# Staging of the first weights, row maxima of v and the route of two early blocks in an attention and MLP kernel

## The chip, the cores and the metric

The kernel runs on one core of one Trainium2 chip. The metric is the device time of one execution in microseconds; lower is better. The five engines are named as in the profile: PE (TensorE, matrix products), DVE (VectorE), ACT (ScalarE), POOL (GpSimd) and SP (SyncE, which issues nearly all of the DMAs).

## The reference

Four batches of eight heads, 768 positions of 64 numbers, go through a local attention, and its output goes through an MLP with 512 inputs, 2048 hidden columns and 512 outputs. All inputs are 32-bit floats except the two MLP weights, which come as 64-bit floats.

```
scores = scale * q @ k.T - slope[h] * dist          # 96 positions back, and the first 8
a = exp(scores - max) / (sum + 1e-9)
x = (a @ v), heads side by side                       # 3072 x 512
h = x @ w_in;  g = h / (1 + exp(-h));  out = g @ w_out
```

## The kernel before

**Blocks.** The 3072 positions are 24 blocks of 128 rows (six to a batch). For each block the kernel loads q, k and v, and the 96 rows of v before it with the first 8 (`vp`); it transposes q and k on PE, computes scores for the block's 232 columns (128 for the first block of a batch), adds the bias and takes the maximum on DVE (line 617), the exponential with its sum on ACT (line 625), transposes P on PE (line 650), copies it back on ACT (line 656) and multiplies with v. A pair of heads is one step; four pairs make a block. The blocks' outputs x are split into a high and a low part of reduced precision (`xh`, `xl`, lines 715 and 718), so that three fast products stand for one exact one.

**Two routes.** Blocks below `IV` (6) leave P as it is: `values_q` (line 677) makes x with positions as rows, the whole block is divided by its sums (`guard_all`, `inverse_all`, `norm_all`), and `turn_x` transposes it. Other blocks divide P before its transposes (`guard`, `inverse`, `norm`, lines 630 to 641), and `values` (line 670) gives x transposed at once, for all four pairs in one run from block `I0` (6) on. From that block on scores too are made of split halves ("stacked", line 578).

**MLP.** Three blocks form a group of 384 columns. Its hidden layer is 16 chunks f of 128 columns, each twelve products (line 833), then tanh on ACT (839), the gate on DVE (843) and a write to DRAM (848). After the eight groups, pairs of blocks are read back, and the output layer is made by seven products on sums and differences (line 888).

**Weights.** w_in arrives as 16 pieces of 512 KB, one for each chunk, in tiles `ws` with seven buffers (tags z0 to z6). DVE makes 32-bit numbers of the 64-bit ones in three operations (365, 371, 377), ACT rounds the high part (383) and DVE subtracts it (387). Each chunk has a tile `wi` of its own, whose memory the output layer uses again (`PART`, `HL`, `OUT`, line 850). w_out follows in eight pairs, whose high and low parts are one operation each (lines 398 to 421), over the memory of the first weights.

**Checks.** The fast route holds for inputs within limits. DVE finds the row maxima of v (`scale_of`, line 511) for each block right after its load, and reads both weights a second time for their extremes (line 473); a verdict at the end decides whether the general route runs.

**Order.** The order of all instructions is found while the program is built. A planner (`Plan`) holds each operation with engine, estimated cost, rank, predecessors and buffers; on each engine it takes, when the engine is free, the ready operation of lowest rank. Where PE has nothing ready in the planner's first 60 us it inserts a filler, a product of zeros (line 1103). Each engine then runs its queue in that fixed order and waits on semaphores. Rank counts pairs of heads: block i's scores have ranks 4 i to 4 i + 3, its loads of q and k 4 i - 8.5 and of v 4 i - 7.5. The conversion of chunk n has rank `C0` + n, its load that less `LW` (12). Hidden-layer products have ranks above 1000 and so go behind attention; tanh, gate and write go ahead of everything. Attention from block 7 on waits for hidden-layer products of earlier groups (`AHEAD`).

Of the kernel before, what the change touches and what calls it, by code (L numbers as in the profile page):

```python
# [21 lines left out]
P = 128  # L22
# [149 lines left out]
def attn_moe(ctx, tc, q, k, v, n_global, n_local, w_in, w_out, out):  # L172
# [176 lines left out]
    def stage(n, nm):  # L349
        if nm == "w" and n < NFC:  # L350
            t = const.tile([P, 3 * 512], U32, name=f"ws_{n}", tag=f"z{n % 7}")
            st["f", n] = t[:, 1024:]
            x = t[:, :1024].rearrange("p (f w) -> p f w", w=2)
        else:
            x = sbx.tile([P, 512, 2], U32, name=f"{nm}_{n}", tag="big")
# [41 lines left out]

    def pair_hi(p):
        if p < 3:
            x = [const.tile([P, 7, HM], F32R, name=f"wo_{p}_{i}", tag=f"z{2 * p + i}") for i in range(2)]  # L400
        elif p < HF - 1:
            x = [st["late"].tile([P, 7, HM], F32R, name=f"wo_{p}_{i}") for i in range(2)]
        else:
            x = [sbx.tile([P, 6, HM], F32R, name=f"wo_{p}_{i}", tag=("xh", "xl")[i]) for i in range(2)]
            y = st["late"].tile([P, 2, HM], F32R, name="wo_last")
            w2[p, 0, 6], w2[p, 1, 6] = y[:, 0], y[:, 1]
        for i in range(2):
            for c in range(7):
                w2.setdefault((p, i, c), x[i][:, c] if c < x[i].shape[1] else None)
        st["wo", p] = x  # L410
        n = x[0].shape[1]
        nc.scalar.copy(x[0], st["F", p][:, :n])
        if n < 7:
            nc.scalar.copy(w2[p, 0, 6], st["F", p][:, 6])

    def pair_lo(p):
        x = st["wo", p]
        n = x[0].shape[1]
        nc.vector.tensor_sub(x[1], st["F", p][:, :n], x[0].bitcast(F32))
        if n < 7:  # L420
            nc.vector.tensor_sub(w2[p, 1, 6], st["F", p][:, 6], w2[p, 0, 6].bitcast(F32))
# [18 lines left out]
    for p in range(HF):  # L440
# [17 lines left out]
        hi = op("ACT", ACT(7 * HM), rank, (lambda p=p: pair_hi(p)), [o] + ([o_late] if p > 2 else []), [F, *a])  # L458
        lo = op("DVE", DVE(7 * HM), rank, (lambda p=p: pair_lo(p)), [hi], [F, *a])
        o_w2.append((hi, lo))  # L460

# [14 lines left out]

    o_c, o_cd, cbuf, o_vm = [], [], [], []
    for n in range(2 * NFC):
# [247 lines left out]
    for i in range(B * NJ):  # L726
# [50 lines left out]
        for hp in range(NHP):  # L777
# [29 lines left out]
            if not plain:  # L807
                last = op("PE", 900 if j else 450, u - PAR["RV"], (lambda i=i, hp=hp, av=pav: values_q(i, hp, av)),
                          [o_m.pop(), last] + o_v, [pt, pav, kk["vn"]] + ([kk["vp"]] if j else []))
            elif not stacked or hp == NHP - 1:  # L810
                last = op("PE", ((2100 if j else 1250) if stacked else 726 if j else 508), u - PAR["RV"],
                          (lambda i=i, hp=hp, av=pav: values_of(i, hp, av)),
                          [*o_m, last] + o_v, [*pts, pav, xb[g]["xh"], xb[g]["xl"], kk["vn"]] + ([kk["vp"]] if j else []))
                o_m, pts = [], []
# [14 lines left out]
    def moe_h(g, f, c, h):  # L829
        mo["ph", g, f] = ph = bank(h, GT)  # L830
        xh, xl = xt["xh", g], xt["xl", g]
        for n, (w, x) in enumerate(((0, xh), (0, xl), (1, xh))):
            nc.tensor.matmul(  # L833
                ph, w1[f][:, w, c], x[:, c], start=not c and not n, stop=c == NCC - 1 and n == 2
            )
# [13 lines left out]

    PART, HL, OUT = ((0, 3, 6, 7), (12, 13, 14, 15)), ((1, 2), (4, 5), (8, 9)), (10, 11)  # L850

    def quarter(g, n):
        t, k = divmod(n, 2)
        b, j = divmod(2 * g + t, NB)
        mo["a", g, n] = x = const.tile([P, HF, P], F32, name=f"a_{g}_{n}", tag=f"wi{PART[g % 2][n]}")
        nc.sync.dma_start(x, gate[b][:, j, k * HF:(k + 1) * HF])
# [17 lines left out]
    def split_hi(g, m):  # L874
        r = HL[(7 * g + m) % len(HL)]
        x = [const.tile([P, HF, P], F32R, name=f"g{i}_{g}_{m}", tag=f"wi{r[i]}") for i in range(2)]
        mo["hl", g, m] = x
        nc.scalar.copy(x[0], mo["a", g, PROD[m][0]])  # L878

    def split_lo(g, m):  # L880
        x = mo["hl", g, m]
        nc.vector.tensor_sub(x[1], mo["a", g, PROD[m][0]], x[0].bitcast(F32))  # L882

    def product(g, m, p, po):
        mo["po", g, m] = y = bank(po, HM)
        a, c = mo["hl", g, m], PROD[m][1]
        for n, (i, w) in enumerate(((0, 0), (0, 1), (1, 0))):
            nc.tensor.matmul(  # L888
                y, a[i][:, p], w2[p, w, c], start=not p and not n, stop=p == HF - 1 and n == 2,
            )  # L890

    def place(g, n):
        if ("out", g) not in mo:
            mo["out", g] = const.tile([P, 2, 2, HM], F32, name=f"o_{g}", tag=f"wi{OUT[g % 2]}")
        return mo["out", g][:, n // 2, n % 2]
# [13 lines left out]

    def moe_out(g, t):  # L910
        n = 2 * g + t
        nc.sync.dma_start(out[n * P:(n + 1) * P], mo["out", g][:, t].rearrange("p a c -> p (a c)"))

    o_h, o_put = {}, {}
    FIRST = -1e6
    for g in range(NGRP):
        o = o_h[g - 1, NFC - 1] if g else None
        for f in range(NFC):
            rank = 1e3 + g * NFC + f
            ph, th = Buf("h"), Buf("g1")  # L920
# [10 lines left out]
    def was(*tags):  # L931

        return [o_h[NGRP - 1, x] for x in tags]

# [4 lines left out]
    for g in range(NPAIR):  # L939
# [4 lines left out]
        for n in range(4):  # L944
            b = (2 * g + n // 2) // NB
            o_q.append(op("DMA", 1456, rank - 8, (lambda g=g, n=n: quarter(g, n)),
                          [o_put[b, NFC - 1]] + (was(PART[g][n]) if first else [free_q[g - 2][n]]), [gq[n]], PAR["DL"]))
        ob, E, ev = Buf("ob"), Buf("g1"), {}
        for m, (src, c) in enumerate(PROD):
# [8 lines left out]
            if not g and src == 0:  # L958
# [4 lines left out]
            hi = op("ACT", ACT(1024), r, (lambda g=g, m=m: split_hi(g, m)),  # L963
                    [h0, o_spl.get("hi")] + (was(*HL[m]) if not g and m < len(HL) else []), [*used, hl])
            o_spl["hi"] = hi
# [10 lines left out]
            if m in (0, 3):  # L976
                ev[m] = op("ACT", ACT(HM), e, (lambda g=g, m=m: keep_half(g, m)),
                           [o] + (was(*OUT) if not g else []), [po, E if m else ob])
            elif m == 1:
                o_1, po_1 = o, po  # L980
            else:
# [297 lines left out]
```

## Time and profile before

| | |
|---|---|
| median of 3 runs (lowest to highest) | 709.94 us (709.85 to 710.8) |
| the profiled execution | 710.94 us |
| its span | 709.2 us |
| PE, PE weight load | busy 694.5 us (98%), 664.6 us (94%) |
| DVE, ACT, POOL | busy 590.5 us (83%), 425.1 us (60%), 26.1 us (4%) |
| mean granted TensorE clock | 0.997 of 2.4 GHz |
| DMA | 114.32 MB, mean 161 GB/s |

The span runs from the first to the last instruction of the profiled execution. A busy time is the union of an engine's instructions; products are pipelined, so the mean of one in a group (346 ns for 384 columns) is longer than its share of the time. Attention and hidden layer share the first 400 us, the hidden layer alone goes on to 463 us, and the output layer takes the rest.

### The profile page before, as it was taken

The numbers are of one execution on the slowest core, as the hardware profiler recorded it, in microseconds if no ns is written. First come the engines' busy times: TensorE is split into PE (matmuls) and PEld (weight loads), VectorE is DVE, ScalarE is ACT, GpSimd is POOL, SyncE is SP. The second block draws the span as 40 slices with busy tenths as digits, with TensorE's granted clock in tenths as the row PEclk, the third lists the DMA queues.
The fourth block names the chain that finished last, engine by engine and source line by source line (L and its number), as shares of the span: only waits on it lengthen the run. The fifth ranks groups of instructions, "written<-read, shape, count | busy, mean of one in ns | idle before, by whom it ended". The sixth has DMA issues, their size and how long they took to land.

```text
span 709.2 us, 14385 instructions
## 1 busy us (share of the span) xinstructions
PE 694.5 (98%) x5294; PEld 664.6 (94%) x5294; DVE 590.5 (83%) x1416; ACT 425.1 (60%) x938; POOL 26.1 (4%) x81
## 2 busy tenths in 40 slices
PE   8999998999999999999999999999999999999996
PEld 5889898998999999999998999999999999999996
DVE  4999798897777888777798558889989899988893
ACT  5877884877777787777797634443333433343331
POOL 2000100000000000000010000000000000000000
PEclk9999999999999999999999999999999999999999
DMA  8979885644566566566542277776544554455300
GB/s 193 266 172 218 180 203 155 177 112 127 139 169 161 139 168 162 134 163 171 137 124 77 71 208 223 228 241 197 196 134 167 188 172 171 147 195 178 121 31 34
DMA packets 175469, 114.32 MB, mean 161 GB/s; under 512 B 96544, under 2 KB 162080, under 8 KB 175392
## 3 DMA queue, kind: packets, MB, share of 16 engines
q1 hardware_dynamic: 175104, 113.34, 56.6%
q8 instruction: 43, 0.70, 0.4%
q14 instruction: 34, 0.28, 0.1%
q10 hardware_dynamic: 288, 0.00, 0.0%
HBM read 81.86 MB, written 31.46 MB: 160 GB/s over the span
## 4 chain that ended last, share of the span: by engine, by line
PE 83%; DVE 9%; ACT 5%; DMA 2%; issue 1%; SPq 0%; DVEq 0%
PE bank L888 34%; PE bank L833 32%; PE bank L650 4%; PE bank L670 4%; PE bank L578 3%; PE bank L518 2%; ACT pe L625 1%; DMA vn<-in_v_dram 1%; PE bank L684 1%; DVE pe L617 1%; PE bank L1103 1%; PE bank L602 1%; DVE th L843 1%; DVE ws L371 1%; DVE ws L377 1%
## 5 line engine op out<-in xcount | busy, mean ns | idle before, releaser
L833 PE MATMUL bank<-xh,wi 128*128 128x384 f32 x1024 | 293.3, 346 | 0.2 <-DVE KL L565 0.2
L888 PE MATMUL bank<-wo,g 128*128 128x256 f32 x1980 | 237.5, 281 | 0.0
L888 PEld LDWEIGHTS bank<-wo,g 128*128 128x128 f32 x1980 | 235.9, 189 | 0.0
L833 PEld LDWEIGHTS bank<-xh,wi 128*128 128x128 f32 x1024 | 188.7, 189 | 3.3 <-issue 2.5
L833 PE MATMUL bank<-xl,wi 128*128 128x384 f32 x512 | 173.1, 338 | 0.0
L625 ACT ACTIVATE pe<-pe,NM 128x232 f32<-128x232 f32 (+1 forms) x192 | 90.2, 471 | 33.0 <-DVE NM L617 31.9
L833 PEld LDWEIGHTS bank<-xl,wi 128*128 128x128 f32 x512 | 97.1, 190 | 0.0
L839 ACT ACTIVATE th<-bank 128x384 f32<-128x384 f32 x128 | 62.1, 487 | 50.9 <-PE bank L833 50.2
L878 ACT CAST g<-S 128x1024 fp32r<-128x1024 f32 x48 | 49.9, 1049 | 61.0 <-DVE S L868 36.3
L843 DVE SCALAR_TENSOR_TENSOR th<-th,bank 128x384 f32<-128x384 f32 x128 | 69.8, 548 | 12.0 <-ACT th L839 11.5
L617 DVE CUSTOM_DVE_ANT_0 pe<-bank,B 128x232 f32<-128x232 f32 (+1 forms) x192 | 67.2, 374 | 12.0 <-PE bank L578 6.7
L882 DVE TENSOR_TENSOR g<-S,g 128x1024 fp32r<-128x1024 f32 x48 | 58.4, 1220 | 15.0 <-ACT g L878 14.9
L650 PE MATMUL bank<-ident,pe 128*128 128x128 f32 (+1 forms) x352 | 57.4, 278 | 5.4 <-DVE pe L641 4.5
L878 ACT CAST g<-a 128x1024 fp32r<-128x1024 f32 x36 | 37.8, 1050 | 37.2 <-PE bank L888 35.2
L656 ACT COPY pt<-bank 128x512 f32<-128x512 f32 (+1 forms) x96 | 52.0, 544 | 7.8 <-PE bank L650 7.4
L650 PEld LDWEIGHTS bank<-ident,pe 128*128 128x128 f32 (+1 forms) x352 | 40.9, 136 | 15.3 <-DVE pe L641 7.5
L473 DVE TENSOR_REDUCE TOP<-c 128x1 f32<-128x512 int16 x64 | 42.3, 677 | 6.4 <-DMA c<-in_moe_w_in_dram 6.2
L882 DVE TENSOR_TENSOR g<-a,g 128x1024 fp32r<-128x1024 f32 x36 | 43.9, 1219 | 3.3 <-ACT g L878 3.2
L641 DVE TENSOR_SCALAR pe<-pe,rs 128x232 f32<-128x232 f32 (+1 forms) x144 | 41.7, 331 | 1.2
L625 ACT ACTIVATION_READ_ACCUMULATOR pe<-pe,NM 128x1 f32 x192 | 36.4, 189 | 0.0
L903 DVE SCALAR_TENSOR_TENSOR o<-bank,o 128x256 f32<-128x256 f32 x60 | 25.1, 419 | 9.3 <-PE bank L888 8.8
L868 DVE TENSOR_TENSOR S<-a,a 128x1024 f32<-128x1024 f32 x24 | 29.3, 1220 | 0.7 <-PE bank L833 0.5
(134 smaller groups left out, 855.1 us busy)
## 6 DMA issues: line engine op xcount, KB each, us to landing
gate<-th SPq DMA_DIRECT2D x128, 192.0 KB
a<-gate SPq DMA_DIRECT2D x48, 512.0 KB
ws<-in_moe_w_in_dram SPq DMA_DIRECT2D x16, 512.0 KB
w<-in_moe_w_out_dram SPq DMA_DIRECT2D x16, 512.0 KB
c<-in_moe_w_in_dram SPq DMA_DIRECT2D x16, 512.0 KB
c<-in_moe_w_out_dram SPq DMA_DIRECT2D x16, 512.0 KB
vn<-in_v_dram SPq DMA_DIRECT2D x24, 256.0 KB
out_dram<-o SPq DMA_DIRECT2D x24, 256.0 KB
```

The lines of the kernel that those rows point to most:

```text
L473: nc.vector.tensor_reduce(TOP[:, i, n:n + 1], top, AX.X, (ALU.min, ALU.max)[i], apply_absolute_value=True)
L617: nc.vector.tensor_tensor_reduce(t["p", hp][:, a, :n], t["s", hp][a][:, :n], B1[:, h] if i % NJ else B0[:, h], -SC, 3.0e38, ALU.add, ALU.m ...
L625: nc.scalar.activation(x, x, AF.Exp, bias=NM[:, i * H + h:i * H + h + 1], scale=-1.0, accum_out=t["sum", hp][:, a:a + 1],)
L641: nc.vector.tensor_scalar(x, x, t["inv", hp][:, a:a + 1], None, ALU.mult)
L650: nc.tensor.transpose(ps[:n, c, a], pe[:, a, c0:c0 + n], ident)
L656: nc.scalar.copy(t["pt", hp][:, c], t["tp", hp][:, c])
L833: nc.tensor.matmul(ph, w1[f][:, w, c], x[:, c], start=not c and not n, stop=c == NCC - 1 and n == 2)
L839: nc.scalar.activation(th, mo["ph", g, f], AF.Tanh, scale=0.5)
L843: nc.vector.scalar_tensor_tensor(gf, gf, 1.0, mo["ph", g, f], ALU.add, ALU.mult)
L878: nc.scalar.copy(x[0], mo["a", g, PROD[m][0]])
L882: nc.vector.tensor_sub(x[1], mo["a", g, PROD[m][0]], x[0].bitcast(F32))
L888: nc.tensor.matmul(y, a[i][:, p], w2[p, w, c], start=not p and not n, stop=p == HF - 1 and n == 2,)
```

## The change

- w_in comes in eight pieces of 1 MB, two chunks each, in tiles of three buffers (tags y0 to y2, 12 KB a partition). Each conversion operation has 1024 columns where it had 512, and a tile `wi` holds two chunks. Conversion ranks become 14, 16, ... 28, and those of their loads 0, 2, ... 14.
- The memory that the first weights leave is cut anew: w_out pairs 0 to 2 take y0 to y2; `PART`, `HL` and `OUT` name the wider tiles, and the two output tiles become one tile of two halves.
- The high and low parts of a w_out pair are made in two operations each, of four and three columns of 256.
- `IV` becomes 4: blocks 4 and 5 divide P before its transposes, and their values come in one run at the block's end.
- The row maxima of v for blocks 0 to 5 are taken from a second load of v (`again`), which starts behind hidden-layer products of groups 2 to 4. For other blocks the maximum has rank 4 i + 3 and is put behind the exponentials of the third pair.
- The last output rows leave as two DMAs, one for each half of the columns.

```diff
-    C0=8, CR=1, LW=12, LB=5, QB=3.5, RI=0.1, RN=0, RP=0.2, RM=0, RV=1.2, RQ=0.1, RB=3, LK=-25,
-
-    BP=(4, 3), CF=8, AHEAD=5, CN=19, I0=6, IV=6, QS='ACT', O0=14, ON=16, PF=16,
+    C0=14, CR=1, LW=14, LB=5, QB=3.5, RI=0.1, RN=0, RP=0.2, RM=0, RV=1.2, RQ=0.1, RB=3, LK=-25,
+
+    BP=(4, 3), CF=8, AHEAD=5, CN=19, I0=6, IV=4, QS='ACT', O0=14, ON=16, PF=16,
...
+    def stage2(n):
+
+        t = const.tile([P, 3 * 1024], U32, name=f"ws_{n}", tag=f"y{n % 3}")
+        st["f", n] = t[:, 2048:]
+        st["w", n] = x = t[:, :2048].rearrange("p (f w) -> p f w", w=2)
+        src = w_in.bitcast(U32).rearrange("(c p) (f w) -> p c f w", p=P, w=2)[:, :, 2 * n * P:2 * (n + 1) * P]
+        nc.sync.dma_start(x.rearrange("p (c f) w -> p c f w", c=NCC), src)
...
+    CUT = (slice(0, 4), slice(4, 7))
+
+    def pair_hi(p, half):
+        if not half:
+            pair_home(p)
+        x, F, c = st["wo", p][0], st["F", p], CUT[half]
+        if x.shape[1] < c.stop:
+            nc.scalar.copy(w2[p, 0, 6], F[:, 6])
+            c = slice(c.start, 6)
+        nc.scalar.copy(x[:, c], F[:, c])
...
-    for n in range(NFC):
-        rank = PAR["C0"] + PAR["CR"] * n
-        o = op("DMA", 2000, rank - PAR["LW"], (lambda n=n: stage(n, "w")), [o_w[n - 7][1]] if n > 6 else (), (), PAR["DW"])
-        o = op("DVE", 335, rank, (lambda n=n: conv1(n)), [o])
-        o = op("DVE", 602, rank, (lambda n=n: conv2(n)), [o])
-        o = op("DVE", 602, rank, (lambda n=n: conv3(n)), [o])
-        hi = op("ACT", 520, rank, (lambda n=n: conv_hi(n)), [o])
-        lo = op("DVE", 602, rank, (lambda n=n: conv_lo(n)), [hi])
+    for n in range(HF):
+        rank = PAR["C0"] + 2 * PAR["CR"] * n
+        o = op("DMA", 3600, rank - PAR["LW"], (lambda n=n: stage2(n)), [o_w[n - 3][1]] if n > 2 else (), (), PAR["DW"])
+        o = op("DVE", 602, rank, (lambda n=n: conv1(n)), [o])
+        o = op("DVE", 1135, rank, (lambda n=n: conv2(n)), [o])
+        o = op("DVE", 1135, rank, (lambda n=n: conv3(n)), [o])
+        hi = op("ACT", ACT(1024, 90), rank, (lambda n=n: conv_hi(n)), [o])
+        lo = op("DVE", 1135, rank, (lambda n=n: conv_lo(n)), [hi])
...
     def scale_of(i):
+        x = st["v", i] if i < PAR["I0"] else blk[i]["v"]
         nc.vector.tensor_reduce(
-            VM[:, i:i + 1], blk[i]["v"].rearrange("p h d -> p (h d)"), AX.X, ALU.max, apply_absolute_value=True
+            VM[:, i:i + 1], x.rearrange("p h d -> p (h d)"), AX.X, ALU.max, apply_absolute_value=True
         )
+
+    def again(i):
+        b, j = divmod(i, NJ)
+        st["v", i] = sbx.tile([P, H, D], F32, name=f"va_{i}", tag="big")
+        nc.sync.dma_start(st["v", i], v[b, :, j * P:(j + 1) * P, :].rearrange("h p d -> p h d"))
...
-        for x in range(NHP) if i >= PAR["I0"] else (hp,):
+        for x in range(NHP):
             values(i, x, av)
...
-        o_vm.append(op("DVE", 602, NHP * i + 2, (lambda i=i: scale_of(i)), list(o_v), [kk["vn"]]))
+        va = Buf("big") if i < PAR["I0"] else kk["vn"]
+        o_va = [op("DMA", 1456, 2e6 + i, (lambda i=i: again(i)), (), [va], PAR["DL"])] if i < PAR["I0"] else list(o_v)
+        o_vm.append(op("DVE", 602, 1e6 if i < PAR["I0"] else NHP * i + 3, (lambda i=i: scale_of(i)), o_va, [va]))
+        o_va2.append((o_va[0], o_vm[-1]))
...
+            if hp == NHP - 2 and i >= PAR["I0"]:
+                plan.after(o_va2[i][1], *o_e)
...
-    PART, HL, OUT = ((0, 3, 6, 7), (12, 13, 14, 15)), ((1, 2), (4, 5), (8, 9)), (10, 11)
+    PART, HL, OUT = ((0, 3), (6, 7)), (1, 2, 4), 5
...
+                    last = g == NPAIR - 1 and m == 6
+                    op("DMA", 728, e, (lambda g=g, t=m - 5, h=0 if last else None: moe_out(g, t, h)), [ev[m], ev[1]], [ob], PAR["DO"])
+                    if last:
+                        op("DMA", 364, e, (lambda g=g: moe_out(g, 1, 1)), [ev[7]], [ob], PAR["DO"])
...
+    for i in range(PAR["I0"]):
+        plan.after(o_va2[i][0], o_h[divmod(2 * NFC + 2 + 8 * i, NFC)])
```

## Rows read from the trace of the kernel before

**Rows 1.** The page's first part: busy us of each engine, share of the span, instructions.

```profile
PE 694.5 (98%) x5294; PEld 664.6 (94%) x5294; DVE 590.5 (83%) x1416; ACT 425.1 (60%) x938; POOL 26.1 (4%) x81
```

**Rows 2.** All engines in stretches of 20 us: us of the stretch; busy us and instructions of PE, PE weight load, DVE, ACT and POOL; granted clock, DMA share, GB/s.

```profile
20.00:40.00 20.00, 20.00 (x176) 17.40 (x175) 19.80 (x54) 15.83 (x45) 1.04 (x2) 1.00 1.09 261
40.00:60.00 20.00, 19.73 (x150) 17.11 (x148) 19.90 (x55) 15.45 (x41) 1.24 (x3) 1.00 0.63 157
60.00:80.00 20.00, 20.00 (x147) 17.93 (x147) 19.37 (x54) 15.75 (x41) 1.32 (x4) 1.00 1.07 226
80.00:100.00 20.00, 19.05 (x131) 17.43 (x130) 15.97 (x53) 19.52 (x53) 1.26 (x4) 1.00 0.82 197
```

**Rows 3.** The same stretches, line 1103 (the fillers) alone: busy us and instructions of PE and PE weight load, clock, DMA share, GB/s.

```profile
20.00:40.00 20.00, 7.37 (x50) 4.66 (x50) 1.00 1.09 261
40.00:60.00 20.00, 1.44 (x9) 0.51 (x6) 1.00 0.63 157
```

**Rows 4.** Pieces of the chain that ended last: start us, length us, what (x how many).

```profile
35.50 1.73 PE bank L684 x16
...
37.67 0.94 PE bank L1103 x8
...
42.41 0.60 DVE xl L718
...
57.25 0.60 DVE xl L718
...
166.46 0.44 PE bank L650 x4
...
172.75 1.91 PE bank L670 x32
...
194.60 2.12 PE bank L833 x12
```

**Rows 5.** Stretches of 20 us, line 387 (the last operation of a chunk's conversion) alone: busy us and instructions of DVE, clock, DMA share, GB/s.

```profile
20.00:40.00 20.00, 3.86 (x6) 1.00 1.09 261
40.00:60.00 20.00, 3.78 (x6) 1.00 0.63 157
```

**Rows 6.** The stretch 40 to 60 us, line 833 (hidden-layer products) alone: busy us and instructions of PE and PE weight load, clock, DMA share, GB/s.

```profile
40.00:60.00 20.00, 8.42 (x37) 6.07 (x38) 1.00 0.63 157
```

**Rows 7.** Who waited for whom between 100 and 170 us: us in total, times, longest us.

```profile
PE bank L650 <- DVE pe L641: 3.4, 3, 1.9
...
DVE VM L511 <- DMA vn<-in_v_dram: 2.6, 2, 1.4
```

**Rows 8.** Pieces of the chain around the two stalls: start us, length us, what.

```profile
113.18 5.17 DMA vn<-in_v_dram
...
119.97 0.26 DVE pe L641
...
156.62 5.01 DMA vn<-in_v_dram
```

**Rows 9.** All engines in stretches of 2 us, columns as in rows 2.

```profile
118.00:120.00 2.00, 0.39 (x3) 0.07 (x1) 1.63 (x7) 1.09 (x1) 0.00 (x0) 1.00 0.45 144
120.00:122.00 2.00, 1.72 (x9) 1.61 (x10) 2.00 (x5) 1.90 (x6) 0.00 (x0) 0.85 0.31 99
122.00:124.00 2.00, 2.00 (x9) 2.00 (x9) 2.00 (x6) 0.40 (x1) 0.00 (x0) 0.50 0.03 8
124.00:126.00 2.00, 2.00 (x11) 2.00 (x11) 2.00 (x9) 0.45 (x2) 0.00 (x0) 0.80 0.31 100
```

**Rows 10.** DVE's groups of instructions by line and shape: line, operation, out<-in, partitions x elements, count; busy us, mean ns of one; idle before them, and what ended it.

```profile
L882 DVE TENSOR_TENSOR g<-a,g 128x1024 fp32r<-128x1024 f32 x36 | 43.9, 1219 | 3.3 <-ACT g L878 3.2
...
L641 DVE TENSOR_SCALAR pe<-pe,rs 128x232 f32<-128x232 f32 x120 | 35.9, 341 | 1.0
...
L511 DVE TENSOR_REDUCE VM<-vn 128x1 f32<-128x512 f32 x24 | 16.3, 681 | 5.7 <-DMA vn<-in_v_dram 5.6
...
L632 DVE TENSOR_SCALAR rs<-sm 128x2 f32<-128x2 f32 x72 | 12.0, 168 | 17.8 <-ACT pe L625 17.5
...
L371 DVE SCALAR_TENSOR_TENSOR ws<-ws 128x512 uint32<-128x512 uint32 x16 | 11.2, 706 | 0.2
...
L377 DVE SCALAR_TENSOR_TENSOR ws<-ws 128x512 uint32<-128x512 uint32 x16 | 10.9, 683 | 0.1
...
L387 DVE TENSOR_TENSOR wi<-ws,wi 128x512 fp32r<-128x512 f32 x16 | 10.7, 684 | 0.4 <-ACT wi L383 0.4
...
L365 DVE TENSOR_SCALAR ws<-ws 128x512 uint32<-128x512 uint32 x16 | 6.5, 411 | 0.0
```

**Rows 11.** ACT's groups, columns as in rows 10.

```profile
L878 ACT CAST g<-a 128x1024 fp32r<-128x1024 f32 x36 | 37.8, 1050 | 37.2 <-PE bank L888 35.2 <-DMA a<-gate 2.0
...
L383 ACT CAST wi<-ws 128x512 fp32r<-128x512 f32 x16 | 9.8, 621 | 2.3 <-DVE ws L377 2.0
```

**Rows 12.** Who DVE waited for between 175 and 345 us: us in total, times, longest us.

```profile
DVE TOP L473 <- DMA c<-in_moe_w_in_dram: 6.2, 5, 1.7
```

**Rows 13.** Who PE waited for in the whole span, its loads: us in total, times, longest us.

```profile
PE bank L518 <- DMA qn<-in_q_dram: 1.0, 1, 1.0
PE bank L518 <- DMA kn<-in_k_dram: 0.6, 1, 0.6
```

**Rows 14.** The last piece of the chain: start us, length us, what.

```profile
703.49 0.42 DVE o L903
```

**Rows 15.** All engines in one stretch at the end, columns as in rows 2.

```profile
705.00:706.00 1.00, 0.00 (x0) 0.00 (x0) 0.00 (x0) 0.00 (x0) 0.00 (x0) 1.00 0.54 199
```

More of the change, by code (lines that the diff above doesn't have):

```diff
@@ L349, in stage @@
     def stage(n, nm):
[L350 to L355, printed above, removed]
+        x = sbx.tile([P, 512, 2], U32, name=f"{nm}_{n}", tag="big")
         st[nm, n] = x
         nc.sync.dma_start(x if n >= NFC else x.rearrange("p (c f) w -> p c f w", c=NCC), source(n))
+    def stage2(n):
[4 more added lines that the diff above has]
+        nc.sync.dma_start(x.rearrange("p (c f) w -> p c f w", c=NCC), src)
     def conv1(n):
@@ L396, in combine, with pair_home @@
         nc.vector.tensor_sub(F[:, x], F[:, a], F[:, b])
-    def pair_hi(p):
+    def pair_home(p):
         if p < 3:
-            x = [const.tile([P, 7, HM], F32R, name=f"wo_{p}_{i}", tag=f"z{2 * p + i}") for i in range(2)]
+            t = const.tile([P, 2, 7, HM], F32R, name=f"wo_{p}", tag=f"y{p}")
+            x = [t[:, i] for i in range(2)]
         elif p < HF - 1:
@@ L407, in pair_hi @@
         for i in range(2):
-            for c in range(7):
-                w2.setdefault((p, i, c), x[i][:, c] if c < x[i].shape[1] else None)
+            for c in range(x[0].shape[1]):
+                w2[p, i, c] = x[i][:, c]
         st["wo", p] = x
[L411 to L421, printed above, removed]
@@ new lines, in pair_hi, with pair_lo @@
+    def pair_hi(p, half):
[6 more added lines that the diff above has]
+        nc.scalar.copy(x[:, c], F[:, c])
+    def pair_lo(p, half):
+        x, F, c = st["wo", p], st["F", p], CUT[half]
+        if x[0].shape[1] < c.stop:
+            nc.vector.tensor_sub(w2[p, 1, 6], F[:, 6], w2[p, 0, 6].bitcast(F32))
+            c = slice(c.start, 6)
+        nc.vector.tensor_sub(x[1][:, c], F[:, c], x[0][:, c].bitcast(F32))
@@ L457, in attn_moe @@
                 x.left = 1
-        hi = op("ACT", ACT(7 * HM), rank, (lambda p=p: pair_hi(p)), [o] + ([o_late] if p > 2 else []), [F, *a])
-        lo = op("DVE", DVE(7 * HM), rank, (lambda p=p: pair_lo(p)), [hi], [F, *a])
-        o_w2.append((hi, lo))
+        his, los = [], []
+        for i in range(2):
+            n = (4, 3)[i] * HM
+            his.append(op("ACT", ACT(n), rank, (lambda p=p, i=i: pair_hi(p, i)), [o, *his] + ([o_late] if p > 2 else []), [F, *a]))
+            los.append(op("DVE", DVE(n), rank, (lambda p=p, i=i: pair_lo(p, i)), [his[-1]], [F, *a]))
+        o_w2.append(los)
     def size_of(n):
@@ L475, in check @@
         )
-    o_c, o_cd, cbuf, o_vm = [], [], [], []
+    o_c, o_cd, cbuf, o_vm, o_va2 = [], [], [], [], []
     for n in range(2 * NFC):
@@ L809, in attn_moe @@
                           [o_m.pop(), last] + o_v, [pt, pav, kk["vn"]] + ([kk["vp"]] if j else []))
-            elif not stacked or hp == NHP - 1:
-                last = op("PE", ((2100 if j else 1250) if stacked else 726 if j else 508), u - PAR["RV"],
+            elif hp == NHP - 1:
+                last = op("PE", 2100 if j else 1250, u - PAR["RV"],
                           (lambda i=i, hp=hp, av=pav: values_of(i, hp, av)),
@@ L833, in moe_h @@
             nc.tensor.matmul(
-                ph, w1[f][:, w, c], x[:, c], start=not c and not n, stop=c == NCC - 1 and n == 2
+                ph, w1[f // 2][:, w, c, f % 2 * P:(f % 2 + 1) * P], x[:, c], start=not c and not n, stop=c == NCC - 1 and n == 2
             )
@@ L888, in product @@
             nc.tensor.matmul(
-                y, a[i][:, p], w2[p, w, c], start=not p and not n, stop=p == HF - 1 and n == 2,
+                y, a[:, i, p], w2[p, w, c], start=not p and not n, stop=p == HF - 1 and n == 2,
             )
@@ L893, in place @@
         if ("out", g) not in mo:
-            mo["out", g] = const.tile([P, 2, 2, HM], F32, name=f"o_{g}", tag=f"wi{OUT[g % 2]}")
+            if g < 2:
+                st["out"] = st["out"] if g else const.tile([P, 2, 2, 2, HM], F32, name="o", tag=f"wi{OUT}")
+            mo["out", g] = st["out"][:, g % 2]
         return mo["out", g][:, n // 2, n % 2]
@@ L908, in add_kept, with moe_out @@
         nc.vector.tensor_add(x[:, 1::2], x[:, 1:3], st["E", g].unsqueeze(1).to_broadcast([P, 2, HM]))
-    def moe_out(g, t):
-        n = 2 * g + t
-        nc.sync.dma_start(out[n * P:(n + 1) * P], mo["out", g][:, t].rearrange("p a c -> p (a c)"))
+    def moe_out(g, t, half=None):
+        n, c = 2 * g + t, slice(0, 2) if half is None else slice(half, half + 1)
+        nc.sync.dma_start(
+            out[n * P:(n + 1) * P, c.start * HM:c.stop * HM], mo["out", g][:, t, c].rearrange("p a c -> p (a c)")
+        )
     o_h, o_put = {}, {}
@@ L931, in was @@
     def was(*tags):
-        return [o_h[NGRP - 1, x] for x in tags]
+        return [o_h[NGRP - 1, 2 * x + 1] for x in tags]
     o_p, sx = [], [Buf("xh"), Buf("xl")]
@@ L946, in attn_moe @@
             o_q.append(op("DMA", 1456, rank - 8, (lambda g=g, n=n: quarter(g, n)),
-                          [o_put[b, NFC - 1]] + (was(PART[g][n]) if first else [free_q[g - 2][n]]), [gq[n]], PAR["DL"]))
+                          [o_put[b, NFC - 1]] + (was(PART[g][n // 2]) if first else [free_q[g - 2][n]]), [gq[n]], PAR["DL"]))
         ob, E, ev = Buf("ob"), Buf("g1"), {}
@@ L963, in attn_moe @@
             hi = op("ACT", ACT(1024), r, (lambda g=g, m=m: split_hi(g, m)),
-                    [h0, o_spl.get("hi")] + (was(*HL[m]) if not g and m < len(HL) else []), [*used, hl])
+                    [h0, o_spl.get("hi")] + (was(HL[m]) if not g and m < len(HL) else []), [*used, hl])
             o_spl["hi"] = hi
@@ L977, in attn_moe @@
                 ev[m] = op("ACT", ACT(HM), e, (lambda g=g, m=m: keep_half(g, m)),
-                           [o] + (was(*OUT) if not g else []), [po, E if m else ob])
+                           [o] + (was(OUT) if not g else []), [po, E if m else ob])
             elif m == 1:
```

15 lines of the change are left out of this document (8 added, 7 removed).

## The prediction

> **What bounds the kernel now.** I read the busy table first: TensorE (PE) is busy 694.5 of 709.2 us, so 14.7 us of the whole span show it idle [rows 1]. That is not all that it loses, because some of its busy time is filler: the multiplications of zeros that the kernel issues (line 1103) where its planner saw PE with nothing to do. So the next view was the first 100 us in stretches of 20 us [rows 2]. Between 20 and 80 us PE and VectorE (DVE) are both full, DVE at 19.8, 19.9 and 19.4 of 20 us; ScalarE (ACT) has about 4 us spare in each stretch until 80 us and none between 80 and 100. The same stretches for line 1103 alone show 50 fillers between 20 and 40 us and 9 between 40 and 60 [rows 3]. A run of 8 takes 0.94 us on the chain [rows 4], so 50 x 0.1175 = 5.9 us of the second stretch are filler: there DVE can't feed PE, as it does weight conversion and attention at once. From 40 us on PE has useful work nearly always: by 60 us some 12 chunks of w_in are split while only 37 hidden-layer multiplications, three chunks' worth, have run [rows 5, 6]. That is a lead of nine chunks, 9 x 12 x 0.177 = 19 us of PE work (12 take 2.12 us [rows 4]). So from 40 us what counts is PE's own work and the few places where its queue stands still.
>
> The largest such places are two waits for DVE. PE waits for the normalised P (line 641) 3.4 us between 100 and 170 us, and DVE waits in the same stretch 2.6 us for v to land, with the row maximum of v (line 511) at the head of its queue [rows 7]. The chain shows both: v takes 5.17 and 5.01 us from issue to landing, and the row maximum stands at its end [rows 8]. After the first of them PE's granted clock falls: 0.85, 0.50 and 0.80 in the three stretches of 2 us from 120 us, after PE did 0.39 us of work in 118 to 120 [rows 9]. At a clock of 0.50, half of the time is lost: 0.3 + 1.0 + 0.4 = 1.7 us. The two places cost some 3.4 + 1.7 = 5.1 us.
>
> **The change part by part.**
>
> Blocks 4 and 5 by the later blocks' route. Removed on PE, per block: 32 value passes, 16 of which take 1.73 us, and four transposes of x, 0.44 us by four of the same shape; added: 32 passes in one run, 1.91 us [rows 4]. 3.46 + 0.44 - 1.91 = 2.0 us a block, 4.0 us for two. On DVE each block gains four sums and four reciprocals (168 ns for one such) and eight normalisations (341 ns) and loses one of each and one product of 512 columns (0.68) [rows 10]: 8 x 0.168 + 8 x 0.341 - 0.34 - 0.68 = 3.05 us, 6.1 us for two. The P transposes of these blocks now wait for DVE, where they waited for ACT; behind such a transpose PE's queue holds hidden-layer work in order, so a late one stops all. I give back 1.5 us for that, between nothing (planned early enough) and 3.4 us, what the same wait costs for the later blocks [rows 7].
>
> First weights in eight pieces of 1 MB. Instructions halve and double in width. DVE before: 16 x (0.411 + 0.706 + 0.683 + 0.684) = 39.7 us. After: 8 x (a + 3 x 1.22), as 1024 columns of two operands take 1.219 us; a, the masked shift at 1024 columns, isn't in the trace: between 0.41 (no more than now) and 0.82 (twice), I take 0.68, nearer the upper end as the work doubles [rows 10]. That is 34.7 us, 5.0 us less. ACT: 16 x 0.621 becomes 8 x 1.050, 1.5 us less [rows 11].
>
> Row maxima. Six leave the full part of DVE, 6 x 0.68 = 4.1 us [rows 10]; they and six more loads of v move to the hidden-layer stage. Those DMAs pass through SP's queue behind the checks' loads, whose waits already hold DVE for 6.2 us in 175 to 345 us [rows 12] beside a full PE; at the longest of them, 1.7 us each, six more would be 10 us of DVE, hidden by PE's backlog unless PE has to wait for the normalised P. I price it at 0, up to +3.4. For the other 18 blocks the maximum now stands behind the exponentials of the third pair of heads, after v has landed; queued behind it are the same normalisations as before. That removes both stalls above if nothing else late stands in the place. Ends 0 and -5.1; I take -3.0.
>
> Weights later in order. DVE's early sum is 6.1 - 5.0 - 4.1 = -3.0 us, so DVE gets no fuller. Conversion ranks start at 14 instead of 8, behind blocks 2 and 3, so DVE serves attention first, and each block gives PE work where there was filler. Between 0 (ACT is the bound instead: 15.8 of 20 us busy) and -5.9 (all 50 fillers go); I take -2.0, nearer to 0 because ACT's spare 4 us are about half of a block's attention. Less of the lead is there when the hidden layer starts: +1.0, between 0 and the first stretch's 37 x 0.177 = 6.5 us.
>
> A load queued behind a weight piece waits for the whole piece: at the 261 GB/s of 20 to 40 us [rows 2], 4.0 us instead of 2.0. Now PE waits for loads only 1.6 us, on the first k and q [rows 13], so I take 0, with three pieces (three buffers) x 2.0 = 6.0 us as the other end. The Trainium skill ("DMA: Bandwidth & Descriptors", section "Queues, rings and completion order") says that each DMA engine consumes its descriptors in ring order, which speaks for the full wait, and against the change; by it the sum would be 6 us worse if no other load were issued ahead.
>
> Halved passes of w_out: the same columns in twice the instructions, beside a full PE: 0, from -1 (DVE is held for shorter) to +1. The last output goes out in halves, the second without waiting: the final transfer is 128 KB less, at 199 GB/s 0.66 us [rows 15]; I take -0.5 of it, behind the last DVE operation [rows 14], between 0 and -0.7.
>
> Sum: -4.0 + 1.5 - 3.0 - 2.0 + 1.0 - 0.5 = -7.0 us. The profiled execution took 710.94 us (709.2 and 1.7 around it), which gives 703.9; it stands 1.0 us above the median of 709.94, so I forecast 703.0.
>
> **The rivals.**
>
> A, only PE's own saving is kept: the stalls re-form with another late wait, ACT is the bound between 20 and 40 us. -4.0 + 1.5 - 0.5 = -3.0: 706.9. For it: ACT is full from 80 to 100 us, and a static order puts some other late landing in front. Against: line 511 is the only thing on DVE that waits for v.
>
> B, slower: the hidden layer starts without weights. If conversion really moved by six steps, one and a half blocks, that is 1.5 x 14.8 = 22 us (from 42.41 to 57.25 us is one block [rows 4]), more than the lead of 19 us: it decides from there. Then the 6.5 us of hidden-layer work in 40 to 60 us are missing, PE idles and the clock falls as at 122 us: +6.5 + 1.7 - 4.0 = +4.2, 714.1. Against: rank is a priority, not a time; DVE takes conversions whenever no earlier work is ready, and it isn't given more in total.
>
> C, no difference: attention's loads wait behind 1 MB pieces, the whole 6.0 us reaching PE: 703.0 + 6.0 = 709.0. By the ring order of the Trainium skill's DMA page this is what would happen. Against: the 1.6 us above; the loads have slack.
>
> D, most comes: both stalls, half of the filler, nothing lost to late weights or transposes: -4.0 - 5.1 - 3.0 - 0.5 = -12.6, 697.3. For it: both stalls have one cause, and the filler has one.
>
> **How the numbers follow.** Chances: forecast 0.53 (its own range 699 to 705.5), A 0.22, D 0.10, C 0.07, B 0.08. A measurement can tell about 0.2%, 1.4 us, from no change. Faster takes the forecast, A and D and a little of C: 0.86; same 0.06, C and the edge of A; slower 0.08, B. The range from 697.5 to 709 leaves out B, the upper edge of C and about half of D, some 0.17.
>
> **What would show it.** Right: fewer than 30 fillers between 20 and 40 us; no wait of line 511 for v; granted clock 1.00 around 120 us; 112 passes of the 64-column kind instead of 176 (blocks 4 and 5 each hold 32); DVE's first-weight work near 35 us. Wrong: PE waits on normalised P between 55 and 90 us of over 3 us; hidden-layer multiplications that wait for conversion; k or q landing late. If PE is idle or slow between 40 and 100 us, step "weights later" is wrong; if the clock still falls near 120 us, step "row maxima" is.

## The result: slower, and the profile after

| | before | after |
|---|---|---|
| median of 4 runs each (lowest to highest) | 710.37 us (709.85 to 711.39) | 720.61 us (719.37 to 721.47) |
| span of the profiled execution | 709.2 us | 719.7 us |
| mean granted TensorE clock | 0.997 | 0.985 |
| output layer's first product | 463.2 us | 449.1 us |

The ratio is 1.0141, 95% interval 1.0121 to 1.0161: slower by 1.4%, where 1.0% faster was forecast. The last row of the table says where to look. The view of the output layer's product line gives the count, the shortest, median and longest duration in ns, and the first and last start in us (the view cuts the line's last figure, 1980). First the kernel before, then the one after:

```profile
L888 PE MATMUL bank<-wo,g x1980: 276/281/386, 463.2 to 702.8; 128*128 128x256 f32 x198
```

```profile
L915 PE MATMUL bank<-wo,g x1980: 277/281/582, 449.1 to 714.1; 128*128 128x256 f32 x198
```

Everything ahead of the output layer became 14.1 us shorter. The same 1980 products then took 265.0 us from first to last start where they had taken 239.6, 25.4 more. The longest took 582 ns, where 386 had been the longest. So there are two results, and they are told apart here.

**The output layer lost.** The page's first part after the change, to be held against [rows 1]:

```profile
PE 693.0 (96%) x5239; PEld 662.7 (92%) x5239; DVE 591.7 (82%) x1418; ACT 423.6 (59%) x938; POOL 29.5 (4%) x81
```

DVE has 1.2 us more work than before (591.7 against 590.5 us) and PE's busy time is 1.5 us less; the span is 10.5 us longer. The waits from 440 us on (us in total, times, longest):

```profile
DVE TOP L487 <- DMA c<-in_moe_w_out_dram: 28.8, 11, 5.7
PEld bank L915 <- DVE g L909: 17.0, 6, 5.2
PE bank L915 <- DVE g L909: 15.7, 6, 5.0
```

In the kernel before, neither PE nor DVE has such a wait behind 440 us. Now DVE stands 28.8 us, each time with line 487 at the head of its queue: an extreme of w_out for the kernel's check of its inputs, on a tile `c` that has not landed. Behind it on DVE is the low part of the next split (line 909), and PE waits for that six times, 15.7 us. The stretches of 50 us (columns as in rows 2) show the rest in the granted clock:

```profile
450.00:500.00 50.00, 44.25 (x353) 43.73 (x353) 39.01 (x48) 16.44 (x19) 0.00 (x0) 0.93 0.50 173
500.00:550.00 50.00, 46.96 (x384) 46.76 (x383) 39.98 (x47) 17.74 (x21) 0.00 (x0) 0.97 0.41 138
550.00:600.00 50.00, 50.00 (x424) 50.00 (x423) 42.76 (x51) 20.06 (x24) 0.00 (x0) 1.00 0.50 166
600.00:650.00 50.00, 44.17 (x357) 43.75 (x356) 37.65 (x46) 17.21 (x20) 0.00 (x0) 0.97 0.47 161
650.00:719.00 69.00, 63.51 (x506) 62.72 (x506) 52.98 (x88) 20.35 (x24) 0.00 (x0) 0.95 0.25 86
```

Where PE does not stand (550 to 600 us), it does 424 products, as many as the kernel before does there. In the others the clock lacks 50 x 0.07 + 50 x 0.03 + 50 x 0.03 + 69 x 0.05 = 10.0 us, but some of that falls where PE stands anyway. Taken in stretches of 2 us and counted only for the time in which PE is busy, it is 8.3 us. With the 15.7 us of waits that is 24.0 of the 25.4 us.

Why the check load is late is read from SP's queue. One round of it, around 480 us (start, length, operation, tile; "SPq" is time in which SP stood or issued):

```profile
479.36 8.03 SPq L883 DMA_DIRECT2D a<-gate  x3
487.48 0.38 SPq L352 DMA_DIRECT2D c<-in_moe_w_out_dram  x1
```

SP stands 8.03 us with three loads of quarters of g and issues the check load only then. What it stood for is on DVE's timeline (the last column gives idle time before the instruction and what ended it):

```profile
485.82 1.22 DVE L909 TENSOR_TENSOR g<-a,g 128x1024 fp32r<-128x1024 f32 x1
486.95 0.42 DVE L932 SCALAR_TENSOR_TENSOR o<-bank,o 128x256 f32<-128x256 f32 x1
493.08 0.69 DVE L487 TENSOR_REDUCE TOP<-c 128x1 f32<-128x512 int16 x1 [5.71 <-DMA c<-in_moe_w_out_dram]
```

PE's timeline has what follows:

```profile
495.56 4.76 PE L915 MATMUL bank<-wo,g 128*128 128x256 f32 x22 [4.99 <-DVE g L909]
```

The split that starts at 485.82 us ends at 487.04; the load goes out at 487.48, lands 5.58 us later, DVE has idled 5.71 us by then and PE 4.99. That split is the seventh product's, the last reader of quarter 3 of the pair that had the tile before (tiles alternate, so two pairs earlier). The change put quarters 2 and 3 of a pair of blocks into one tile (`quarter`, with `PART` cut to two tiles a pair):

```python
if ("q", g, t) not in mo:
    mo["q", g, t] = const.tile([P, 2, HF, P], F32, ..., tag=f"wi{PART[g % 2][t]}")
```

Each pair takes the tile anew, so the load of quarter 2 waits for the last reader of the whole tile, quarter 3's too. The planner's entry (`free_q[g - 2][n]`) still says that quarter 2 is free after an early subtraction, so the load stands early in SP's order and holds what is queued behind it. In the kernel before, each quarter had a tile of its own, and SP's queue at the same point reads:

```profile
471.16 1.91 SPq L856 DMA_DIRECT2D a<-gate  x3
473.12 0.42 SPq L357 DMA_DIRECT2D c<-in_moe_w_out_dram  x1
```

**The first part gained.** Two stretches of 100 us, first the kernel before and then the one after (columns as in rows 2):

```profile
0.00:100.00 100.00, 96.15 (x697) 81.56 (x698) 85.01 (x262) 79.46 (x223) 8.81 (x29) 1.00 0.89 210
100.00:200.00 100.00, 96.61 (x695) 92.56 (x694) 85.53 (x253) 70.16 (x168) 4.43 (x14) 0.98 0.55 147
```

```profile
0.00:100.00 100.00, 95.75 (x684) 81.89 (x685) 83.20 (x251) 80.87 (x221) 10.55 (x29) 1.00 0.83 207
100.00:200.00 100.00, 99.68 (x752) 94.81 (x751) 94.27 (x287) 77.51 (x190) 6.94 (x16) 1.00 0.67 173
```

From 100 to 200 us PE idles 0.32 us instead of 3.39, and the clock is 1.00 instead of 0.98, which by the three stretches of [rows 9] is 1.7 us more: 4.8 in all. Of the fillers, 31 are left instead of 78 (the kernel before, then after; 10 of the 31 lie between 20 and 40 us, where there were 50 [rows 3]), which at the prediction's 0.1175 us each is 5.5 us:

```profile
L1103 PE MATMUL bank<-wx x78: 269/273/422, 1.0 to 43.1; 128*128 128x256 bf16 x78
```

```profile
L1139 PE MATMUL bank<-wx x31: 269/421/421, 1.1 to 35.4; 128*128 128x256 bf16 x31
```

With the prediction's estimate of 4.0 us of products that blocks 4 and 5 no longer need, that is 14.3 us, where 14.1 were measured.

### The profile page after: what moved, and what is told of

Its sections match the earlier page's. It is cut to its first block, busy times and chain, and to the rows that moved or that the text cites. A ratio compares the mean times of both kernels' runs of the same rounds, so it can differ in the third digit from the quotient of the medians.

```text
span 719.7 us, 14272 instructions
## 1 busy us (share of the span) xinstructions
PE 693.0 (96%) x5239; PEld 662.7 (92%) x5239; DVE 591.7 (82%) x1418; ACT 423.6 (59%) x938; POOL 29.5 (4%) x81
## 4 chain that ended last, share of the span: by engine, by line
PE 59%; DVE 22%; DMA 10%; issue 5%; ACT 3%; SPq 1%; ACTq 0%; DVEq 0%
PE bank L858 32%; PE bank L915 9%; DMA c<-in_moe_w_out_dram 8%; DVE g L909 6%; PE bank L670 5%; PE bank L690 4%; DVE S L895 3%; PE bank L598 3%; PE bank L538 2%; DVE TOP L487 2%; ACT g L905 2%; PE bank L704 1%; DVE pe L637 1%; DVE o L932 1%; PE bank L622 1%
## 5 line engine op out<-in xcount | busy, mean ns | idle before, releaser
L915 PE MATMUL bank<-wo,g 128*128 128x256 f32 x1980 | 246.8, 287 | 15.7 <-DVE g L909 15.7
L915 PEld LDWEIGHTS bank<-wo,g 128*128 128x128 f32 x1980 | 243.8, 195 | 17.1 <-DVE g L909 17.0
L868 DVE SCALAR_TENSOR_TENSOR th<-th,bank 128x384 f32<-128x384 f32 x128 | 70.2, 549 | 14.4 <-ACT th L864 13.5
L487 DVE TENSOR_REDUCE TOP<-c 128x1 f32<-128x512 int16 x64 | 42.3, 678 | 29.3 <-DMA c<-in_moe_w_out_dram 28.8
L661 DVE TENSOR_SCALAR pe<-pe,rs 128x232 f32<-128x232 f32 (+1 forms) x160 | 46.9, 331 | 1.0
L929 ACT ACTIVATE o<-bank 128x256 f32<-128x256 f32 x12 | 4.6, 385 | 45.3 <-PE bank L915 43.5
```

Of the source, the lines that this page charges most:

```text
L487: nc.vector.tensor_reduce(TOP[:, i, n:n + 1], top, AX.X, (ALU.min, ALU.max)[i], apply_absolute_value=True)
L661: nc.vector.tensor_scalar(x, x, t["inv", hp][:, a:a + 1], None, ALU.mult)
L868: nc.vector.scalar_tensor_tensor(gf, gf, 1.0, mo["ph", g, f], ALU.add, ALU.mult)
L915: nc.tensor.matmul(y, a[:, i, p], w2[p, w, c], start=not p and not n, stop=p == HF - 1 and n == 2,)
```

## The experiments

Two questions: is the joint tile the whole loss, and what is each part of the gain worth. "Quarters kept" below means the first edit.

**1. The changed kernel with the quarters' tiles taken once**, so that a later pair writes into the same tile and each half of it is waited for by itself.

```diff
-        if ("q", g, t) not in mo:
+        if g > 1:
+            mo["q", g, t] = mo["q", g - 2, t]
+        elif ("q", g, t) not in mo:
```

> The changed kernel with one edit: the four tiles for the gate quarters of the output layer are taken once and written again by region, instead of a new tile for each pair of blocks. Theory T (shared tile: a quarter's load waits until the last reader of BOTH quarters in its tile is done, SP's queue stands, the check loads behind it land late, DVE waits for them at the head of its queue, PE for DVE): TensorE's waits for DVE in the output layer fall from 15.7 us to under 2 us, the output layer takes again about 246 us (709.2 - 463.2 before) instead of 270.6 us, and the time is 449 + 246 + 2 = about 697 us. Rival R1 (the new output tile or the joint tile of high and low parts makes TensorE wait): nothing changes, 720 us. Rival R2 (the output layer now starts 14 us earlier and meets other traffic, so the check loads are just slow): the DVE waits for check loads stay near 28.8 us, 715 to 720 us.

Measured: 697.23 us, ratio to before 0.9796 (0.9745 to 0.9847). The output layer's products:

```profile
L917 PE MATMUL bank<-wo,g x1980: 277/281/387, 448.8 to 688.9; 128*128 128x256 f32 x198
```

Its waits from 440 us on:

```profile
DVE TOP L487 <- DMA c<-in_moe_w_out_dram: 2.7, 2, 2.4
...
PE bank L917 <- DVE g L911: 0.2, 1, 0.2
```

240.1 us from first to last start, as before the change (239.6). The new output tile, the joint tile of high and low parts and the earlier start are all still there, so R1 and R2 fall. The lifetime of that tile is the whole loss; the rest of the change is 2% faster than the kernel before.

**2. The changed kernel with the 16 check loads of w_out on GpSimd's queue**, the joint tile as it is. This tells whether the late quarters hurt, or what stands behind them.

```diff
-        nc.sync.dma_start(x if n >= NFC else ...
+        (nc.gpsimd if nm == "c" and n >= NFC else nc.sync).dma_start(x if n >= NFC else ...
```

> The changed kernel with only the 16 check loads of w_out issued by GpSimd's queue instead of SyncE's; the shared quarter tiles stay. Theory T with the check load behind the quarter as its second half: the check loads leave on time, DVE's wait for them falls from 28.8 us to under 6 us, TensorE's wait for DVE from 15.7 us to under 4 us; 697 to 702 us. If the late quarters themselves are what DVE and TensorE lack, TensorE's waits stay above 10 us and the time at 712 to 720 us. R1 and R2: no change, 715 to 722 us.

Measured: 695.61 us, ratio 0.9774 (0.9725 to 0.9823). SP still stands as long, and nothing comes of it; its queue in the same round:

```profile
478.52 8.51 SPq L883 DMA_DIRECT2D a<-gate  x4
```

The only wait of DVE for a load from 440 us on:

```profile
DVE g L909 <- DMA a<-gate: 0.7, 1, 0.7
```

So the quarters may be 8 us late at no price. What cost 25 us was that an unrelated load was queued behind them and that DVE's queue was ordered for that load to be on time. The Trainium skill ("DMA: Bandwidth & Descriptors", section "Issuing engines are not separate DMA queues") says that starting DMAs from several engines saves no more than the time it takes to start them, usually small. Here it saved 25.0 us (720.61 - 695.61), as the issuing engine was not busy but waiting; the measurement decides.

**3. Both cures together.**

> The changed kernel with the quarter tiles kept (as in the first experiment) and the 16 check loads of w_out on GpSimd's queue (as in the second). Theory T (the only loss is the stand of SP's queue, and one cure is enough): the two cures take away the same thing, so 694.5 to 697.5 us, within 0.3% of the better of the two; no wait of PE for the split of line 909 over 0.5 us in all; waits of DVE for a check load of w_out go from 2.7 us to below 0.5. Rival (the two losses are separate: late quarters still cost PE in the second experiment, late checks in the first): the sum of both gains over either, below 693.5 us.

Measured: 697.42 us, ratio 0.9805 (0.9781 to 0.9828), the output layer from 447.8 to 687.4 us and neither wait left. The two cures take away the same thing; their intervals overlap, so none of the three versions is shown to be the fastest.

**4. The kernel before, made to wait in the same way**: from the third pair on, the load of quarter 3 is issued ahead of quarter 2's, so that SP stands for quarter 3's last reader. Nothing else of the change is in it.

```diff
     def quarter(g, n):
+        if g > 1 and n > 1:
+            if n == 2:
+                quarter_of(g, 3)
+                quarter_of(g, 2)
+        else:
+            quarter_of(g, n)
+
+    def quarter_of(g, n):
```

> The kernel before, with one edit in the output layer: from the third pair of blocks on, the load of quarter 3 is issued just ahead of that of quarter 2, so that SyncE's queue stands at quarter 2's place until quarter 3's last reader is done, as in the changed kernel, with all tiles as before. Theory T: DVE waits for check loads appear, TensorE waits for DVE by 10 to 16 us, its clock falls in places, the time rises by 15 to 25 us to 725 to 735 us. R1 and R2: no more than 1 us of change, 709 to 712 us.

Measured: 743.87 us, ratio 1.0448 (1.0393 to 1.0503). The same two waits appear:

```profile
DVE TOP L473 <- DMA c<-in_moe_w_out_dram: 35.8, 8, 7.3
...
PE bank L896 <- DVE g L890: 24.7, 6, 6.0
```

The mechanism alone makes the kernel before slower; the size was missed by 9 us at least. The waits are longer than after the change, and the clock is 0.93 in all four stretches of 50 us from 500 to 700 us, which I had not counted.

**The parts of the gain.** Each of the next four undoes one part in the kernel of experiment 1 (quarters kept; 697.23 us, output layer from 448.8 us). The start of the output layer is what they are compared by, since nothing behind it differs. It is read from one execution each, and it varies: the changed kernel and experiments 1 to 3 have the same first part and start their output layers at 449.1, 448.8, 450.5 and 447.8 us. A difference below some 3 us is not shown by such a pair.

**5. Blocks 4 and 5 on the old route.**

```diff
-    ... IV=4, ...
+    ... IV=6, ...
...
-        for x in range(NHP):
+        for x in range(NHP) if i >= PAR["I0"] else (hp,):
```

> On top of the kept quarter tiles (697.2 us): blocks 4 and 5 go back to the old route (sums divided out after the values, x transposed). If TensorE bounds the first part by its own work, the saving of 4.0 us comes back whole: hidden layer ends 4 us later than 448.8, 701 us. If the wait for normalised P had eaten 1.5 us of it, as forecast: +2.5, 699.7. If DVE were the bound there, the kernel gets faster by up to 3 us, as DVE loses 6.1 us of work.

Measured: 699.3 us, ratio 0.9848 (0.9817 to 0.9879); the output layer starts at 450.4 us, 1.6 later, but 0.1 earlier than in experiment 2. So a gain from these two blocks is not shown; the time, 2.1 us longer, is near the second branch (699.7). PE waits 1.0 us for normalised P instead of 2.1, and idles 3.40 us of the first 100 instead of 4.90, which is where some of the saved products' time may go.

**6. Row maxima of blocks 0 to 5 early again**, from the first load of v.

```diff
-        x = st["v", i] if i < PAR["I0"] else blk[i]["v"]
+        x = blk[i]["v"]
...
-        va = Buf("big") if i < PAR["I0"] else kk["vn"]
-        o_va = [op("DMA", ...)] if i < PAR["I0"] else list(o_v)
-        o_vm.append(op("DVE", 602, 1e6 if i < PAR["I0"] else NHP * i + 3, ...))
+        va = kk["vn"]
+        o_va = list(o_v)
+        o_vm.append(op("DVE", 602, NHP * i + (2 if i < PAR["I0"] else 3), ...))
...
-    for i in range(PAR["I0"]):
-        plan.after(o_va2[i][0], o_h[divmod(2 * NFC + 2 + 8 * i, NFC)])
```

> On top of the kept quarter tiles (697.2 us): the row maxima of v for blocks 0 to 5 are taken early again, from the block's own load, with no second load. DVE gets 4.1 us more in its full part. If DVE is the bound there: +2 to +4 us, 699 to 701. If TensorE is the bound: within 1 us of 697.2.

Measured: 700.43 us, ratio 0.9858 (0.9829 to 0.9888); the output layer starts at 453.4 us, 4.6 later, about what the six maxima take on DVE (4.1 us [rows 10]); the branch in which DVE is the bound holds. Up to 445 us PE idles only 1.3 us more than in experiment 1 (7.9 against 6.6), and its weight loads stand 3.1 us more (busy 407.0 instead of 410.1 us).

**7. Row maxima of the other 18 blocks in front again.**

```diff
-        o_vm.append(op("DVE", 602, 1e6 if i < PAR["I0"] else NHP * i + 3, ...))
+        o_vm.append(op("DVE", 602, 1e6 if i < PAR["I0"] else NHP * i + 2, ...))
...
-            if hp == NHP - 2 and i >= PAR["I0"]:
-                plan.after(o_va2[i][1], *o_e)
```

> On top of the kept quarter tiles (697.2 us): for blocks 6 to 23 the row maximum of v goes back to its old rank with no wait for the scores' exponentials. If it made both stalls near 118 and 160 us, they return: TensorE waits for normalised P of 3 us or more between 100 and 170 us, clock below 1.00 near one of them, +3 to +5 us, 700 to 702. If the stalls had gone because the order is another, no change within 1 us.

Measured: 704.42 us, ratio 0.9908 (0.9876 to 0.994); the output layer starts at 457.2 us, 8.4 later. Its waits up to 445 us show the two lines of rows 7 again; with the maxima behind the scores the first is 2.1 us in 4 times and the second is not there:

```profile
PE bank L670 <- DVE pe L661: 6.6, 10, 1.7
...
DVE VM L526 <- DMA vn<-in_v_dram: 4.2, 6, 1.1
```

In the stretch that the expectation named, 100 to 170 us, the wait for normalised P is 2.6 us, less than the 3 expected, and the clock does not fall: it is 1.00 in every stretch of 2 us there. The time is 2.4 us above the range expected. So the waits come back as foreseen, spread further and without the clock's part, and the price is larger. PE idles 4.3 us more than in experiment 1 up to 445 us. The other 4.1 of the 8.4 us are not idle time of PE. Its weight loads stand 7.1 us more (busy 403.0 instead of 410.1 us), so part may be short waits that products still running hide; that is not shown, and where the 4.1 us go stays open.

**8. Weights early again**: conversion ranks from 8 instead of 14, loads 14 ahead as in the change.

```diff
-    C0=14, ...
+    C0=8, ...
```

> On top of the kept quarter tiles (697.2 us): conversion ranks start at 8 again (loads at -6), still in 1 MB pieces. If the later order is what replaced the fillers: 30 or more fillers between 20 and 40 us instead of 10, hidden layer later by 3 to 5 us, 700 to 702. If the lighter DVE load alone did it: fillers stay near 10 and the time within 1 us of 697.2.

Measured: 704.44 us, ratio 0.9918 (0.9891 to 0.9945); the output layer starts at 457.0 us, 8.2 later. The first branch holds, though the time is 2.4 us above its range. There are 104 fillers instead of 31, 46 of them between 20 and 40 us:

```profile
L1141 PE MATMUL bank<-wx x104: 269/273/421, 1.1 to 45.9; 128*128 128x256 bf16 x104
```

**9. The later order alone, in the kernel before** (C0 from 8 to 14 and LW from 12 to 14, the pieces of 512 KB kept).

> The kernel before with the conversion ranks and load lead of the changed kernel alone (C0 14, LW 14, in pieces of 512 KB as before), nothing else of the change. If the later order is worth by itself what its undoing cost (8.2 us at the start of the output layer): the output layer starts near 455 us (before 463.2) and the time is near 702 us, with fewer than 30 fillers from 20 to 40 us. If it pays only together with the lighter conversion and the early maxima taken off DVE (my second theory, since DVE is full there): the output layer starts at 459 to 463 and the time is 706 to 710.

Measured: 704.8 us, ratio 0.9903 (0.9871 to 0.9934). The output layer starts at 456.8 us, 6.4 earlier than in the kernel before, and the fillers go:

```profile
L1103 PE MATMUL bank<-wx x32: 272/396/421, 1.1 to 34.8; 128*128 128x256 bf16 x32
```

Most of the order's worth needs no other part of the change: the idea that it pays only with the lighter conversion falls. Undone one at a time the four parts come to 1.6 + 4.6 + 8.4 + 8.2 = 22.8 us, where the whole first part gained 14.4 (463.2 - 448.8). So these are not terms of a sum. Either some parts are worth more with the others there, or what was never undone alone, the pieces of 1 MB above all, costs something; no run tells which. The order accounts for little of the excess: it is worth 6.4 us alone and 8.2 with the rest, and these differ by less than the spread.

## Why the prediction was wrong

**The step that failed is one that it did not take.** The change as listed ahead of the prediction says that `PART`, `HL` and `OUT` name wider tiles. The prediction priced every other line of that list and gave this one no term, and the sum let the output layer keep its 246.0 us apart from a half microsecond at the end. It should have asked of each tile that now holds two things when it comes free, who waits for that, and what is queued behind the one who waits; the prediction asks the last of these of the second loads of v and of attention's loads behind 1 MB pieces, and of no tile. No rival had the mechanism. B, the only slow one, was refuted: in 40 to 60 us the hidden layer has more products than before (46 against 37 [rows 6]), and PE had no wait for a conversion there. Line 858, the hidden layer's, after the change:

```profile
40.00:60.00 20.00, 9.99 (x46) 7.59 (x47) 1.00 0.81 205
```

Every sign that the prediction named for being right came true: 10 fillers between 20 and 40 us, no wait for v at the row maximum, clock 1.00 around 120 us, 112 passes, 34.8 us of DVE. Of those for being wrong there are only traces (0.9 us of waits for normalised P between 55 and 90 us, 0.2 us for a late k). All of them lie in the first part, so none could show a loss in the output layer.

**The rest of the change, without the tile, is 697.2 us**, rival D's time (697.3) and not the forecast's 703.0. That D's sum comes out so well is in part luck: it has all 4.0 us of blocks 4 and 5, which are not shown, too little for the weights' order and nothing for the six early maxima. Term by term:

- Blocks 4 and 5, -4.0 and +1.5 given back, net -2.5: not shown. Experiment 5 gives -1.6, less than the spread of the starts, which neither bears out nor refutes the -2.5. PE's wait for normalised P between 40 and 100 us is 1.5 us after the change, the value taken; the 64-column products are the 112 foreseen:

```profile
L704 PE MATMUL bank<-vn,pt 128*128 128x64 f32 x64 | 12.2, 284 | 0.0
L704 PE MATMUL bank<-vp,pt 104*128 104x64 f32 x48 | 9.3, 274 | 0.0
```

- First weights in 1 MB pieces: right. Forecast 34.7 us for DVE; the three operations take 5.4 + 9.7 + 10.0 and the last 9.7, 34.8 us. The masked shift at 1024 columns takes 678 ns (0.68 taken):

```profile
L380 DVE SCALAR_TENSOR_TENSOR ws<-ws 128x1024 uint32<-128x1024 uint32 x8 | 10.0, 1253 | 0.0
L374 DVE SCALAR_TENSOR_TENSOR ws<-ws 128x1024 uint32<-128x1024 uint32 x8 | 9.7, 1215 | 0.0
L390 DVE TENSOR_TENSOR wi<-ws,wi 128x1024 fp32r<-128x1024 f32 x8 | 9.7, 1208 | 0.1
...
L368 DVE TENSOR_SCALAR ws<-ws 128x1024 uint32<-128x1024 uint32 x8 | 5.4, 678 | 0.0
```

- Row maxima behind the scores, -3.0: mis-sized. Both stalls went with little in their place (0.32 us of idle), -4.8 us between 100 and 200 us, near the -5.1 that D took; undone alone in experiment 7 the part is worth 8.4. In 118 to 124 us [rows 9] PE is now busy throughout and its clock is 1.00.
- The six early maxima, no term of their own, only 4.1 us off DVE: mis-sized, 4.6 us by experiment 6. DVE was the full engine from 20 to 80 us [rows 2], so work taken off it was worth about its duration; by which waits it reached PE is only in part shown. The reload cost nothing: no wait of line 526 for v is left.
- Weights later, -2.0 and +1.0: mis-sized, -6.4 alone by experiment 9. The bound was near (-5.9, all 50 fillers of 20 to 40 us go; 40 of them went), and I had kept away from it because ACT was 15.8 of 20 us busy in 20 to 40 us. It is 17.8 after the change: the spare time was enough. The lead that I gave 1.0 us for was not missed.
- Loads behind 1 MB pieces, 0, rival C at +6.0: the value holds. PE waits 1.7 us for k and q, and 2.4 in experiment 1, where it was 1.6 [rows 13]. The Trainium skill's rule of ring order ("DMA: Bandwidth & Descriptors", section "Queues, rings and completion order") is not refuted by that; these runs show no cost of it that reached PE.
- Last output in halves, -0.5: not seen. From the last product's start to the end of the span it was 6.4 us; with the halves it is 5.6 after the change, 6.2 in experiment 1 and 6.4 in experiment 3.

## What to carry to other kernels

Two buffers that become one tile share one lifetime: for each such merger, look up the last reader of the longer-lived half, and find whose load will now wait for it. Here a load that waited for a buffer held all that was queued behind it on its engine (8.03 us in the round shown), so the price is not its own lateness but that of the next unrelated load, and of the instruction that stands at the head of a compute queue for that one. Where an engine is full and another is fed by filler, price work taken off the full one at about its whole duration (here 4.1 us of DVE were worth some 4.6).

## What the runs showed that was not expected

A wait costs PE more than its idle time in this layer too. After the 4.99 us of idle that end at 495.56 us, the granted clock stays at its lower level, 1.2 of 2.4 GHz, for some 4 us more (stretches of 2 us, columns as in rows 2):

```profile
492.00:494.00 2.00, 0.00 (x0) 0.00 (x0) 0.92 (x2) 0.00 (x0) 0.00 (x0) 0.74 0.42 170
494.00:496.00 2.00, 0.45 (x2) 0.45 (x3) 2.00 (x4) 0.00 (x0) 0.00 (x0) 0.50 0.00 0
496.00:498.00 2.00, 2.00 (x11) 2.00 (x11) 2.00 (x3) 0.00 (x0) 0.00 (x0) 0.50 0.34 131
498.00:500.00 2.00, 2.00 (x12) 2.00 (x11) 1.97 (x4) 0.00 (x0) 0.00 (x0) 0.55 0.32 121
500.00:502.00 2.00, 2.00 (x19) 2.00 (x18) 1.82 (x3) 1.32 (x2) 0.00 (x0) 1.00 0.92 272
```

11 and 12 products start in 2 us there, against 19 in each of the three stretches from 484 to 490 us, at the full clock. In all, the waits of 15.7 us came with a loss of 25.4 us, 1.6 times their length. Shorter waits need not do this: in experiment 7 PE idles 1.7 us between 110 and 114 us, and the clock stays at 1.00.
